# Two heads to a task: K tiles that hold half of each of two heads, and V in rows of 8 KB

## The chip, the cores and the metric

One core of a Trainium2 chip runs the whole program. The metric is the device time of one execution in microseconds; before the change three runs took 1159.95, 1160.93 and 1161.16 us, median 1160.93.

The five engines are TensorE (PE, with PEld for its weight loads), VectorE (DVE), ScalarE (ACT), GpSimd (POOL) and SyncE (SP). SP issues every DMA of this kernel, in one queue and in order; 16 DMA engines move the bytes.

## What is computed

A decode step of a transformer with two layers, each attention and an MLP, both layers with the same weights and the same K and V caches. There are 8 sequences (batches) with one new token each, width 512, 32 query heads in 8 groups on 8 K/V heads, 8192 cached positions, head size 128, all bf16.

```python
def _A_ref(x, k_cache, v_cache, wq, wo):          # k_cache, v_cache: (8, 8, 8192, 128)
    q = (x @ wq).reshape(B, Sq, Hq, Dh).transpose(0, 2, 1, 3)
    k = jnp.repeat(k_cache, 4, axis=1)
    v = jnp.repeat(v_cache, 4, axis=1)
    p = _softmax(jnp.einsum("bhqd,bhkd->bhqk", q, k) * (Dh ** -0.5), axis=-1)
    o = jnp.einsum("bhqk,bhkd->bhqd", p, v)
    return o.transpose(0, 2, 1, 3).reshape(B, Sq, Hq * Dh) @ wo
def _B_ref(x, w1, w2):
    return _silu(x @ w1) @ w2                     # 512 -> 1792 -> 512
for _layer in range(2):
    x = x + _A_ref(_layernorm(x), k_cache, v_cache, wq, wo)
    x = x + _B_ref(_layernorm(x), w1, w2)
```

K and V of one batch and head are 2 MB each. All K and V together are 268 MB, and layer 2 needs them again.

## The kernel before

**Tasks and positions.** A task is one layer, batch and K/V head: 2 x 8 x 8 = 128 tasks. A task has 8 *positions* (GPT); two positions make a *granule* (GPG), and a task has four granules, each 2048 cached keys. The program is one loop over positions p (L1010 of the listing), which emits for all engines what belongs to p.

**The arena.** K and V land in ARENA, 28 slots of 512 KB (4 KB in each of 128 partitions). A granule of K or of V takes one slot. Of each batch, K of heads 3 to 7 (20 granules) is *kept* in the arena from layer 0 until layer 1 has scored it, so it is read once; heads 0 to 2 are read in both layers. The kept K of heads 3 to 7 in layer 0 comes as one load of 2 MB with 16 KB rows. V of a granule is one load of 512 KB with 4 KB rows.

**Order of tasks** (`make_tasks`). For each batch b: layer 0 of heads 3 to 7 (here the *kept stretch*: wide K and V are loaded), then some five tasks of heads 0 to 2, of layer 0 of later batches and layer 1 of earlier ones (the *middle stretch*: K and V in 512 KB loads), then layer 1 of heads 3 to 7 (the *late stretch*: V alone is loaded, and kept K is given back). The chain from layer 0 to layer 1 of a batch (wo, residual, layer norm, w1, silu, w2, residual, layer norm, wq; some twenty stages, one or more in a position) runs within the middle stretch.

**Loads** (`plan_loads`). Every load has a position `need` at which it is used and one, `free`, at which its slot comes free. Loads are sorted by `need`; each gets the slot that comes free first and a position `after` from which it may be issued. SP issues in this order (`issue_until`), and waits where the slot is still in use; what stands behind it waits too. K is needed a position ahead of its granule, V LP = 14 positions behind it.

**One task.** K of a granule is transposed in place in 32 x 32 blocks by VectorE (L497). PE multiplies it with the queries (L563) into one of two PSUM banks SCp; a bank is 128 x 512, its 64 used rows are (column group, granule, head of the group). After the last granule: row maximum (L574), its spread over the 4 query heads (L576), an all-reduce over partitions on POOL (L579), the shift (L583, L586), exp on ACT into P (L590), sums (L597, POOL L599), four transposes on PE into TPp (L608), copy to PT (L612). Then P times V (L628), a granule each time two positions have passed, into one of two banks OTp. The four column groups of the result are joined: ACT writes the first part into `joint` (L643), VectorE adds three (L651), PE folds the rows (L665), VectorE scales (L675). P and `joint` are the same tile E.

The positions of these steps within a task are fixed: softmax_max at 0 (of the next task's positions), shift and exp at 2, sum at 4, turning P at 5, reciprocal at 7; own at 6, join at 7, fold and norm at 1, each LP + GPT positions behind the task.

Of the kernel before, what the change touches and what calls it, by code (L numbers as in the profile page):

```python
# [19 lines left out]
READ = (1, 1, 1, 4, 4, 4, 4, 4)  # L20
KEEP = 20
LT = 1
PRE = 10
LP = 14
EARLY = 4
DEAL_AT = 30
WO_FROM = 36
NTP = 2
NSCP = 2
NPT = 1  # L30
# [12 lines left out]
NAT = 2  # L43
CW = 32
# [108 lines left out]

def make_tasks(nb, nkv, keep_from):
# [10 lines left out]
    na = 0  # L165
    for b in range(nb):
        if b:
            tasks += kept[b]
        size = -(-(2 * first * (nb - 1)) // nb) if b in (0, nb - 1) else 2 * first * (nb - 1) // nb
        must = max(0, first * min(b + 1, nb - 1) - na)  # L170
        nd = size if b == nb - 1 else min(len(behind), first, size - must)
        tasks += behind[:nd]
        del behind[:nd]
        take = ahead[na:na + size - nd]
        na += len(take)
        tasks += take
        if b + 1 == nb:
            tasks += behind
        tasks += c[b]
        behind += d[b]  # L180
# [4 lines left out]
def plan_loads(tasks, kept, nslot, ngran):  # L185
# [3 lines left out]
    for i, (layer, b, g) in enumerate(tasks):  # L189
        for k in range(ngran):  # L190
# [8 lines left out]
            loads.append(Load("V", b, g, k, i0 + GPG - 1 + LP, i0 + GPG - 1 + LP))  # L199
    loads.sort(key=lambda d: (d.need, d.kind))  # L200
# [8 lines left out]
    for d in loads:  # L209
        w = ngran if d.kind == "K" and (d.g, d.k) in kept else 1  # L210
        if w > 1 and d.k:
            d.slot = whole[d.g] + d.k
            d.after = by
            assert d.after < d.need or d.need == -1 and d.after == -2, (d.kind, d.need, d.after)
            continue
# [5 lines left out]
        for m in range(w):  # L221
            free[d.slot + m] = d.free
        if w > 1:
            whole[d.g] = d.slot
# [19 lines left out]
def _build(ctx, nc, A_x, A_k_cache, A_v_cache, A_wq, A_wo, B_w1, B_w2, out):  # L244
# [43 lines left out]
    def half(slot, h):  # L288
# [8 lines left out]
    XT = [sb([128, KT, B], BF16, f"XT{n}") for n in range(3)]  # L297
# [5 lines left out]
    QT2 = [sb([128, HQ], BF16, "QT2") for _ in range(2)]  # L303
# [12 lines left out]
    hsT = sb([128, FT * B], BF16, "hsT")  # L316
    xnT = sb([128, KT, B], BF16, "xnT")
    s1 = sb([128, B], FP32, "s1")
    s1a = sb([128, B], FP32, "s1a")
    s2 = sb([128, 1], FP32, "s2")  # L320
    s2a = sb([128, 1], FP32, "s2a")
    top = sb([128, REP], FP32, "top")
    tops = sb([128, REP], FP32, "tops")
    ssm = [sb([128, REP], FP32, "ssm") for _ in range(NST)]
    ssa = [sb([128, REP], FP32, "ssa") for _ in range(NST)]
    widths = {"own_q": NQ, "hm": REP, "far": REP, "mine": REP, "own_x": XW, "real": 1, "rowmax": 1,
              "eps": 1, "shift": 1, "eh": FT, "vr": B, "yr": B, "tr": B}
    widths.update({f"rcp{n}": REP for n in range(NST)})
    widths.update({f"rs{n}": 1 for n in range(NST)})
    row = sb([128, sum(widths.values())], FP32, "row")  # L330
    tiny, at_col = {}, 0
    for name, w in widths.items():
        tiny[name] = row[:, at_col:at_col + w]
        at_col += w
    own_q, hm, far, mine, own_x, real, rowmax, eps, shift, vr, yr, tr = (
        tiny[n] for n in ("own_q", "hm", "far", "mine", "own_x", "real", "rowmax", "eps", "shift", "vr", "yr", "tr"))
    rcp = [tiny[f"rcp{n}"] for n in range(NST)]
    rs = [tiny[f"rs{n}"] for n in range(NST)]

# [58 lines left out]
    def issue(d):  # L398
        cache = A_k_cache if d.kind == "K" else A_v_cache
        if d.kind == "K":  # L400
            src = cache[d.b, d.g].rearrange("(p k c) d -> k p (c d)", k=NGRAN // d.wide, p=128)[d.k // d.wide]
        else:
            src = cache[d.b, d.g].rearrange("(k p c) d -> k p (c d)", k=NGRAN, p=128)[d.k]
# [7 lines left out]
    with nc.Block() as block:  # L411

        @block.sync
        def _(sync_eng):
# [13 lines left out]
                    hm[:, :], lanes.rearrange("p c (k r) -> p r c k", k=NGRAN), AX.XY, ALU.add),  # L428
                reads=["ident"], writes=["hm"],
            )  # L430
            op(
# [7 lines left out]
            for n in range(NSCP):  # L439
                op(dve, lambda n=n: dve.memset(SCp[n][:, :], 0.0), writes=[f"SC{n}"])  # L440
            op(dve, lambda: dve.tensor_reduce(real[:, :], hm[:, :], AX.X, ALU.add), reads=["hm"], writes=["real"])
# [3 lines left out]
            op(dve, lambda: dve.tensor_scalar(  # L445
                far[:, :], hm[:, :], real[:, 0:1], FAR, op0=ALU.subtract, op1=ALU.mult),
               reads=["hm", "real"], writes=["far"])
# [57 lines left out]

            span_of = {}
# [10 lines left out]
            def emit_queries(layer, b):  # L517
                if layer == 0:
                    q, rq = QT1[:, b * HQ:(b + 1) * HQ], f"QT1_{b}"
                else:  # L520
                    q, rq = QT2[b % 2][:, :], f"QT2_{b % 2}"
# [9 lines left out]
            def emit_q(ti):  # L531
                layer, b, g = tasks[ti]
                if ti == span_of[(layer, b)][0]:
                    emit_queries(layer, b)
                n = ti % NQB
                at = qset[(layer, b)] * NPART * HQ
                op(dve, lambda: dve.tensor_tensor(  # L537
                    QB[n][:, :, :].rearrange("p i (a r) -> p i a r", a=NQ),
                    QSp[:, at:at + NPART * HQ].rearrange("p (i h) -> p i h", h=HQ)[:, :, g * REP:(g + 1) * REP].unsqueeze(2)
                    .to_broadcast([128, NPART, NQ, REP]),  # L540
                    own_q[:, :].unsqueeze(1).unsqueeze(3).to_broadcast([128, NPART, NQ, REP]), ALU.mult),
                   reads=["QS", "own_q"], writes=[f"QB{n}"])

            def emit_s(i):
# [9 lines left out]
                bank, qn = ti % NSCP, ti % NQB  # L554
# [17 lines left out]
            def softmax_max(ti):  # L572
                bank = ti % NSCP
                op(dve, lambda: dve.tensor_reduce(rowmax[:, :], SCp[bank][:, :], AX.X, ALU.max),  # L574
                   reads=[f"SC{bank}"], writes=["rowmax"])
# [434 lines left out]
            for p in range(NG + LP + GPT + FOLD + 1):  # L1010
# [22 lines left out]
                if 0 <= ti < ntask and ph in soft:  # L1033
                    for f in soft[ph]:
                        f(ti)
# [62 lines left out]
```

## Time and profile before

| | |
|---|---|
| median of three runs | 1160.93 us |
| the profiled execution, its own time | 1159.96 us |
| its span, first to last instruction | 1157.8 us |
| what lies around the span | 2.2 us |
| busy: PE, PEld, DVE, ACT, POOL | 725.2, 346.7, 740.8, 336.6, 116.7 us |
| mean granted TensorE clock | 0.596 of full speed |
| HBM read | 465.05 MB, 402 GB/s over the span |
| transposes of K (L497) | 352, 1235 ns each |
| exp (L590) | 128, 1421 ns each (with the read of its sum) |
| row maximum (L574) | 128, 659 ns each |
| all-reduces on POOL (L579, L599) | 128 and 128, 371 and 436 ns each |

How to read it: busy time is the time in which an engine has an instruction at work, over the whole span; the page also gives it in 40 equal slices as digits, tenths of a slice. A group's line has the line of the code, engine, operation, what it writes and reads, the count, its busy time, the mean of one, and then the engine's idle time just ahead of it with what ended that idle time. A DMA group has KB of one load and the median time from issue to landing. In the list of waits stand the waiting engine and line, the releaser, the total, how often, and the longest.

### The profile page before, as it was taken

To read this page: it belongs to the slowest core of one execution; us is meant where nothing else is said; L and a number is where in the kernel's file an instruction comes from. 1 tells how busy PE (TensorE), PEld (TensorE's weight loads), DVE (VectorE), ACT (ScalarE), POOL (GpSimd) and SP (SyncE) were. 2 spreads that over 40 slices of the span, in tenths; PEclk is the share of its full clock that TensorE was granted. 3 is DMA by queue.
4 is the path that set the end of the run, shared out by engine and by line. 5 is a ranking of instruction groups with operands and counts; after the bars stand their busy time and mean duration, and the time that the engine had idled before them with its cause. 6 is when DMAs were issued, how large, how long until landed. Compare 5 with 4: busy or idle time off the path is not lost.

```text
span 1157.8 us, 26616 instructions
## 1 busy us (share of the span) xinstructions
PE 725.2 (63%) x10768; PEld 346.7 (30%) x10768; DVE 740.8 (64%) x1781; ACT 336.6 (29%) x764; POOL 116.7 (10%) x296
## 2 busy tenths in 40 slices
PE   1445677566765676567756676567665677567666
PEld 1212342123322342134322342134222332134224
DVE  3836764676557675677467765677477755677464
ACT  0352224223332233122422233222332233223332
POOL 0000011001110111001100011001100011001110
PEclk9855556555765566555755576555755565556665
DMA  9999999999999999999999999999999999999994
GB/s 372 403 400 415 408 408 414 417 411 404 407 419 415 402 407 417 419 401 409 408 416 411 409 401 416 417 407 403 406 419 410 409 401 419 414 408 403 409 408 184
DMA packets 112602, 466.80 MB, mean 403 GB/s; under 512 B 11984, under 2 KB 16096, under 8 KB 106720
## 3 DMA queue, kind: packets, MB, share of 16 engines
q1 hardware_dynamic: 112480, 465.11, 100.1%
q8 instruction: 85, 1.39, 0.5%
q14 instruction: 37, 0.30, 0.1%
HBM read 465.05 MB, written 0.01 MB: 402 GB/s over the span
## 4 chain that ended last, share of the span: by engine, by line
DMA 53%; DVE 15%; PE 13%; SPq 9%; issue 6%; ACT 3%; POOL 1%; DVEq 0%; ACTq 0%; POOLq 0%
DMA arena<-in_A_v_cache_dram 36%; DMA arena<-in_A_k_cache_dram 17%; SPq L379 9%; DVE arena L497 6%; DVE E L651 4%; PE OTp L628 4%; PE SCp L563 3%; DVE row L574 2%; PE TPp L608 2%; PE OTp L665 1%; PE MISC L762 1%; ACT E L590 1%; PE MISC L780 1%; ACT PT L612 1%; DVE top L576 1%
## 5 line engine op out<-in xcount | busy, mean ns | idle before, releaser
L497 DVE STREAM_TRANSPOSE arena<-arena 128x1024 int32<-128x1024 int32 x352 | 433.3, 1235 | 162.2 <-DMA arena<-in_A_k_cache_dram 161.9
L628 PE MATMUL OTp<-arena,PT 128*16 128x512 bf16 (+1 forms) x2064 | 278.5, 550 | 292.3 <-DMA arena<-in_A_v_cache_dram 271.3
L590 ACT ACTIVATE E<-SCp,row 128x512 bf16<-128x512 f32 x128 | 181.9, 1421 | 605.9 <-DVE row L586 587.2
L563 PE MATMUL SCp<-arena,QB 128*16 128x128 bf16 (+1 forms) x4352 | 251.1, 375 | 22.6 <-DVE arena L497 16.3
L651 DVE SCALAR_TENSOR_TENSOR E<-OTp,row,E 128x128 f32<-128x128 f32 x381 | 130.2, 342 | 113.6 <-ACT E L643 103.1
L628 PEld LDWEIGHTS OTp<-arena,PT 128*16 128x16 bf16 (+1 forms) x2064 | 51.2, 92 | 422.0 <-DMA arena<-in_A_v_cache_dram 382.6
L563 PEld LDWEIGHTS SCp<-arena,QB 128*16 128x16 bf16 x4352 | 100.8, 110 | 112.2 <-issue 59.2
L579 POOL PARTITION_ALL_REDUCE tops<-top x128 | 47.5, 371 | 587.7 <-DVE top L576 439.0
L608 PE MATMUL TPp<-ident,E 128*128 128x128 bf16 x512 | 72.7, 291 | 37.6 <-ACT E L590 36.2
L599 POOL PARTITION_ALL_REDUCE ssa<-ssm x128 | 55.8, 436 | 350.2 <-ACT ssm L597 350.2
L574 DVE TENSOR_REDUCE row<-SCp 128x1 f32<-128x512 f32 x128 | 84.4, 659 | 0.7 <-PE SCp L563 0.7
L612 ACT COPY PT<-TPp 128x256 bf16<-128x256 bf16 x128 | 47.7, 372 | 125.0 <-PE TPp L608 125.0
L665 PE MATMUL OTp<-row,E 128*128 128x4 f32 x254 | 68.9, 342 | 23.3 <-DVE E L651 23.2
L665 PEld LDWEIGHTS OTp<-row,E 128*128 128x128 f32 x254 | 57.8, 283 | 82.9 <-DVE E L651 47.3
L608 PEld LDWEIGHTS TPp<-ident,E 128*128 128x128 bf16 x512 | 41.1, 124 | 111.5 <-ACT E L590 89.5
L780 PE MATMUL MISC<-at,wo 128*128 128x32 bf16 x1024 | 37.4, 188 | 18.8 <-DVE row L583 14.7
L643 ACT ACTIVATE E<-OTp,row 128x128 f32<-128x128 f32 x127 | 47.2, 372 | 0.0
L762 PE MATMUL MISC<-xnT,wq 128*128 128x32 bf16 (+1 forms) x1152 | 35.8, 186 | 14.2 <-DVE xnT L749 13.9
L762 PEld LDWEIGHTS MISC<-xnT,wq 128*128 128x128 bf16 x1152 | 34.8, 105 | 20.8 <-issue 18.6
L780 PEld LDWEIGHTS MISC<-at,wo 128*128 128x128 bf16 x1024 | 32.9, 105 | 25.4 <-DVE at L675 22.3
L597 ACT ACTIVATE ssm<-row 128x4 f32<-128x4 f32 x128 | 37.9, 296 | 3.8
L537 DVE TENSOR_TENSOR QB<-QSp,row 128x64 bf16<-128x64 f32 x128 | 25.7, 201 | 17.6 <-PE QSp L524 17.5
(100 smaller groups left out, 319.3 us busy)
## 6 DMA issues: line engine op xcount, KB each, us to landing
arena<-in_A_v_cache_dram SPq DMA_DIRECT2D x512, 512.0 KB, 10.5
arena<-in_A_k_cache_dram SPq DMA_DIRECT2D x192, 512.0 KB, 8.3
arena<-in_A_k_cache_dram SPq DMA_DIRECT2D x40, 2048.0 KB, 22.5
wq<-in_A_wq_dram SPq DMA_DIRECT2D x1, 4096.0 KB, 16.3
wo<-in_A_wo_dram SPq DMA_DIRECT2D x1, 4096.0 KB, 36.9
w<-in_B_w_dram SPq DMA_DIRECT2D x2, 1792.0 KB, 25.0
E<-in_A_x_dram SPq DMA_DIRECT2D x1, 8.0 KB
out_dram<-E SPq DMA_DIRECT2D x1, 8.0 KB
```

What stands on the lines that cost most here:

```text
L379: eng.dma_start(out_ap, in_ap).then_inc(counter.sem, 16)
L497: op(dve, lambda: dve.transpose(words, words), reads=[r_half(slot, 0), r_half(slot, 1)], writes=[r_half(slot, 0), r_half(slot, 1)])
L563: lambda n=n, t=t: pe.matmul(SCp[bank][t * QUAD:t * QUAD + USED, lo * 128:(lo + len(slots)) * 128], QB[qn][:, n, :], keys(t, n), start=(n ...
L574: op(dve, lambda: dve.tensor_reduce(rowmax[:, :], SCp[bank][:, :], AX.X, ALU.max), reads=[f"SC{bank}"], writes=["rowmax"])
L590: op(act, lambda: act.activation(P[:, :].rearrange("p (x j k) -> p k x j", x=CPB, k=NGRAN), SCp[bank][:, :].rearrange("p (k x j) -> p k x ...
L608: lambda c=c: pe.transpose(tpv[:, c, :], P[:, c * 128:(c + 1) * 128], ident[:, :])
L612: op(act, lambda: act.copy(PT[pb][:, :, :, :, :].rearrange("p a t x r -> p x t a r"), tpv.rearrange("p x (t q) -> p x t q", q=QUAD)[:, :, ...
L628: lambda t=t, y=y: pe.matmul(OTp[ob][t * QUAD:t * QUAD + w * REP, 0:w * DH], PT[pb][:, k, t, y * w:(y + 1) * w].rearrange("p x r -> p (x r)"),
L651: op(dve, lambda x=x: dve.scalar_tensor_tensor(joint, OTp[ob][:, x * DH:(x + 1) * DH], own_x[:, x:x + 1], joint, op0=ALU.mult, op1=ALU.add ...
L665: lambda: pe.matmul(OTp[ob][:, 0:REP], joint, hm[:, :], start=True, stop=True)
L762: lambda o=o, k=k: pe.matmul(MISC[:, o * n:o * n + w], w_sb[:, k, o * 128:(o + 1) * 128], rhs_of(k).to_broadcast([128, w]) if n == 1 else ...
L780: lambda o=o, h=h: pe.matmul(MISC[:, o * w:(o + 1) * w], wo_sb[:, h, o * 128:(o + 1) * 128], rhs_of(h).to_broadcast([128, w]) if n == 1 el ...
```

## The change

Heads 0 and 1, 4 and 5, 6 and 7 become pairs (DUOS); heads 2 and 3 stay alone. A pair is two tasks in a row.

- **K of a pair.** A K tile no longer holds 128 rows of one head. Partitions 0 to 63 hold rows of the first head, 64 to 127 rows of the second; a partition's whole row is 128 keys (32 KB) and a tile takes every eighth part of it (4 KB), or for kept K half of it (16 KB). So a pair's eight tiles together hold both heads, and none can be finished before both tasks are scored. The number and size of the K loads stay.
- **V of a pair** is loaded two granules at once: 1 MB with 8 KB rows, into two slots next to each other. The second slot comes free two positions after the first.
- **Scores** of a pair lie in two banks, so there are three (NSCP), and one bank TPp is given up, of which both halves are now used. A kept head of a pair is scored by `score_both` in two groups of 16 matmuls with 256 columns, in place of one group of 16 with 512.
- **Softmax** is done once for a pair, in the first eight positions after its second task: two row maxima, one all-reduce over 8 columns in place of two over 4, two exps through the same P with a turn between them, two copies to PT (NPT = 2). The sum of a pair is formed on VectorE and no longer on ACT. A head alone waits the same eight positions more.
- **Lags.** V lags 22 positions (LP) in place of 14. The queries of the first late task are now due at position 4 of that task (LATE), not 3 before it.
- **Order.** `make_tasks` doesn't part a pair; the middle stretches have 5, 6, 5, 5, 5, 6, 4 and 6 tasks, before 6, 5, 5, 5, 5, 5, 5 and 6.
- **Room.** XT has one buffer in place of three, QT2 one in place of two; small tiles move into `row`, E and a free slot of the arena.

The diff, cut to its core:

```diff
+DUOS = (0, 4, 6)
-LP = 14
+LP = 22
-NTP = 2
-NSCP = 2
-NPT = 1
+NTP = 1
+NSCP = 3
+NPT = 2
+LATE = 4
...
+def lead_of(g):
+    return g - 1 if g - 1 in DUOS else g
+
+def members(g):
+    return 2 if lead_of(g) in DUOS else 1
...
-            loads.append(Load("V", b, g, k, i0 + GPG - 1 + LP, i0 + GPG - 1 + LP))
-    loads.sort(key=lambda d: (d.need, d.kind))
+            w = members(g)
+            if k % w == 0:
+                loads.append(Load("V", b, g, k, i0 + GPG - 1 + LP, i0 + GPG - 1 + LP, w))
+    loads.sort(key=lambda d: (d.need, d.kind == "K" and d.wide == 1))
...
         for m in range(w):
-            free[d.slot + m] = d.free
+            free[d.slot + m] = d.free + (GPG * m if d.kind == "V" else 0)
...
         if d.kind == "K":
-            src = cache[d.b, d.g].rearrange("(p k c) d -> k p (c d)", k=NGRAN // d.wide, p=128)[d.k // d.wide]
+            rows = cache[d.b, lead:lead + n].rearrange("g (p f) d -> (g p) (f d)", p=128 // n)
+            at = own if d.wide > 1 else d.k * n + own
+            src = rows[:, at * d.wide * SLOT:(at + 1) * d.wide * SLOT]
         else:
-            src = cache[d.b, d.g].rearrange("(k p c) d -> k p (c d)", k=NGRAN, p=128)[d.k]
+            src = cache[d.b, d.g].rearrange("(k p c) d -> k p (c d)", k=NGRAN // n, p=128)[d.k // n]
...
+            def score_both(ti, slots, qn):
+                own = tasks[ti][2] - lead_of(tasks[ti][2])
+                cols = NGRAN // 2 * 128
+                many = ARENA[:, slots[0] * SLOT:(slots[0] + NGRAN) * SLOT].rearrange(
+                    "p (k u t x h j e) -> p u t h e k x j", u=2, t=NQ, x=CPB, h=PAIRS, e=2, j=QUAD)
+                for u in range(2):
+                    bank = (ti - own + u) % NSCP
+                    mm_group([
+                        lambda n=n, t=t: pe.matmul(
+                            SCp[bank][t * QUAD:t * QUAD + USED, own * cols:(own + 1) * cols], QB[qn][:, n, :],
+                            many[:, u, t, n // 2, n % 2], start=(n == 0), stop=(n == NPART - 1))
+                        for n in range(NPART) for t in range(NQ)
+                    ], reads=[r_half(slot, h) for slot in slots for h in range(2)] + [f"QB{qn}"], writes=[f"SC{bank}"])
...
+                for n in range(many):
+                    bank = (ti + n) % NSCP
+                    op(dve, lambda: dve.tensor_reduce(rowmax[:, n:n + 1], SCp[bank][:, :], AX.X, ALU.max),
+                       reads=[f"SC{bank}"], writes=["rowmax"])
+                if many > 1:
+                    op(dve, lambda: dve.tensor_tensor(rowmax[:, 0:1], rowmax[:, 0:1], rowmax[:, 1:2], ALU.max),
+                       reads=["rowmax"], writes=["rowmax"])
...
-            soft = {0: [softmax_max], 2: [softmax_shift, softmax_exp], 4: [softmax_sum], 5: [emit_pt], 7: [softmax_rcp]}
...
+            def softmax(ti, ph):
+                many = members(tasks[ti][2])
+                if ph == 0:
+                    softmax_max(ti)
+                elif ph == 2:
+                    softmax_shift(ti)
+                    softmax_exp(ti, 0)
+                elif ph == 3 and many > 1:
+                    emit_turn(ti, 0)
+                    softmax_exp(ti, 1)
+                elif ph == 4:
+                    softmax_sum(ti)
+                elif ph == 5:
+                    emit_turn(ti, many - 1)
+                    emit_pt(ti)
+                elif ph == 7:
+                    softmax_rcp(ti)
...
-                ob, pb = ti % 2, ti % NPT
+                ob, own, many = ti % 2, g - lead_of(g), members(g)
+                pb, at = (ti - own + k % many) % NPT, own * NGRAN // many + k // many
...
-                        PT[pb][:, k, t, y * w:(y + 1) * w].rearrange("p x r -> p (x r)"),
+                        PT[pb][:, at, t, y * w:(y + 1) * w].rearrange("p x r -> p (x r)"),
...
-                ti, ph = p // GPT - 1, p % GPT
-                if 0 <= ti < ntask and ph in soft:
-                    for f in soft[ph]:
-                        f(ti)
+                ti = p // GPT - 2
+                if 0 <= ti < ntask and lead_of(tasks[ti][2]) == tasks[ti][2]:
+                    softmax(ti, p % GPT)
                 if chain:
-                    left = max(1, first1[chain_b[0]] - EARLY - p)
+                    left = max(1, due_of[first1[chain_b[0]]] + LQ - EARLY - p)
```

`emit_turn` makes the four PE transposes of P that `emit_pt` made before, into one half of TPp; `emit_pt` copies one half or both to PT.

## The prediction

> **What bounds the kernel now.** I read the profiled execution from the outside in: slices, DMA queues, stretches, then the waits. The first two views say that the DMA engines never rest.
>
> ```profile
> span 1157.8 us, 26616 instructions
> ...
> DMA  9999999999999999999999999999999999999994
> GB/s 372 403 400 415 408 408 414 417 411 404 407 419 415 402 407 417 419 401 409 408 416 411 409 401 416 417 407 403 406 419 410 409 401 419 414 408 403 409 408 184
> DMA packets 112602, 466.80 MB, mean 403 GB/s; under 512 B 11984, under 2 KB 16096, under 8 KB 106720
> ...
> q1 hardware_dynamic: 112480, 465.11, 100.1%
> ...
> arena<-in_A_v_cache_dram SPq DMA_DIRECT2D x512, 512.0 KB, 10.5
> arena<-in_A_k_cache_dram SPq DMA_DIRECT2D x192, 512.0 KB, 8.3
> arena<-in_A_k_cache_dram SPq DMA_DIRECT2D x40, 2048.0 KB, 22.5
> ```
>
> No slice but the last falls below 90%, and q1 alone fills the 16 engines. No compute engine does: PE is 63% and VectorE (DVE) 64% busy. The waits point the same way:
>
> ```profile
> PEld OTp L628 <- DMA arena<-in_A_v_cache_dram: 382.6, 291, 16.8
> ...
> DVE arena L497 <- DMA arena<-in_A_k_cache_dram: 161.9, 83, 7.3
> ```
>
> P·V waits for V and the transposes for K. So the time is the packet work of the DMA queue, plus a start, plus the 14 us between the last data packet (1143.9 us) and the end. The rate isn't flat, and that is where the row length shows (columns: stretch, busy times, PE clock, DMA share, GB/s):
>
> ```profile
> 9.40:19.40 10.00, 0.24 (x4) 0.18 (x4) 2.93 (x12) 0.00 (x0) 0.28 (x1) 1.00 1.00 418
> 54.00:64.00 10.00, 0.00 (x0) 0.00 (x0) 0.59 (x1) 9.14 (x3) 0.00 (x0) 0.50 1.10 348
> 110.00:180.00 70.00, 49.62 (x904) 27.44 (x900) 47.83 (x115) 19.11 (x50) 7.57 (x19) 0.52 1.03 408
> 191.00:241.00 50.00, 28.53 (x270) 10.27 (x258) 31.54 (x70) 14.10 (x30) 4.43 (x11) 0.57 1.02 417
> ```
>
> These are wq (8 KB rows), wo (1 KB rows), K and V in 4 KB rows, and wide K (16 KB rows) with V, half and half.
>
> **1. V in 8 KB rows.** Six of eight heads are in pairs: 6 x 8 x 2 = 96 tasks, 384 loads of 512 KB, which become 192 of 1 MB: 201 MB. Per engine 3072 packets of 4 KB become 1536 of 8 KB, so 1536 go. Price of one packet, with one engine at a sixteenth of the rate: 4 KB at 408 GB/s is 160.6 ns. wo: 1 KB at 348 is 47.1 ns, and four of these less 160.6, over three packets, are 9.2 ns. Kept stretch: 157.2 ns per 4 KB at 417 means 153.8 for the 16 KB half, and 6.8 ns over three quarters of a packet are 9.1. wq: 313.6 ns per 8 KB at 418, against 321.2, is 7.6. The packet records have medians of 160 ns (4 KB) and 309 ns (8 KB): 11. So 7.6 to 11 ns, 11.7 to 16.9 us. I take 9.5, between wo's and the records: **-14.6 us**.
>
> The Trainium skill, "DMA: Bandwidth & Descriptors", section "Why small descriptors are slow (HBM only)", gives a packet a fixed overhead of some 3 cycles beside one per 32 B: 262 cycles for two packets of 4 KB, 259 for one of 8 KB. By it the 201 MB would save 1.1% of their 493 us, an estimate of 5.6 us. The four rows above all say more, so the trace doesn't agree.
>
> **2. K in halves.** The 32 tasks of heads 0 and 1 still read 4 KB rows, the kept ones 16 KB rows; only the row pitch doubles. K (16 KB pitch) and V (contiguous) land 1.28 us apart alike at 110 to 180 us, so I charge 0; 1 ns on each of 1024 packets per engine would be 1 us, either way.
>
> **3. The arena behind a pair.** This is the new risk. Twenty of 28 slots hold kept K, eight circulate. Carrying out the planner of both versions: in the middle stretch (heads 0 to 2 of either layer) the loads issued but not yet needed are a constant 7 slots before; after, they alternate between 5 and 7, since a pair is given back only when its second half is used, two positions on. One round is a V pair A and K tiles k1, k2: 2.49 + 2 x 1.28 = 5.05 us of DMA. A lands at 0, k1 at 1.28; k1 is transposed (1.24, L497), scored (0.60, L563), then A's second half is used (0.60, L628): with 0.2 of semaphores A is free at 3.9. VectorE may be late: from landing to the next issue on its slot a K tile is held 2.45, 3.11, 2.45 and 3.95 us in turn (trace, 112 to 135 us; V 0.74). The tiles that gate a pair are the first and third of a task, so up to 0.65 more: 4.6. Six slots (7.5 us) were queued when A landed, 2.9 us of them remain. A new load needs 1.04 us to its first packet and 0.72 us from last packet to count (first load: issued 0.79, first packet 1.83, first engine 3.83), so 1.1 us of cover is left at worst, 1.7 at best: **0 us** in a steady round. SP's queue is in order, so the K loads behind a pair wait with it; that is in these numbers.
>
> **4. The chain of stages to layer 1** (wo, MLP, query; once in each of the eight middle stretches) puts PE behind: at 797 to 809 us K is held 5.06 and 3.86, V 1.5 to 2.8, some 1.5 to 2 us over steady. That was hidden by a queue deeper by one slot; now it exceeds the cover by 0 to 0.9. I take 0.5 each, **+4 us**; bounds 0 and 14 (1.75 each, the whole mean lag). It now has 18 positions where it had 19 (due 4 after the first late task, start 8 later), once only 10.
>
> **5. Softmax in pairs.** Two exponentials share one P buffer: PE's first turn waits for exp 0, exp 1 on ScalarE (ACT) for that turn; the next K score and P·V queue behind it on PE, and SP waits for those. In the middle stretch two positions take 2.57 us against 1.43 + 0.27 + 0.6 (L590, L608), so nothing stalls. In the late stretch (layer 1, heads 3 to 7) compute sets its own pace, 5.7 us a task:
>
> ```profile
> 824.83 1.12 DVE L651 SCALAR_TENSOR_TENSOR E<-OTp,row,E 128x128 f32<-128x128 f32 x3 [2.85 <-ACT E L643]
> 825.87 0.17 DVE L619 RECIPROCAL row<-ssa 128x4 f32<-128x4 f32 x1
> 825.96 0.66 DVE L574 TENSOR_REDUCE row<-SCp 128x1 f32<-128x512 f32 x1
> 826.65 0.22 DVE L576 SCALAR_TENSOR_TENSOR top<-row 128x4 f32<-128x4 f32 x1
> ...
> 830.57 1.13 DVE L651 SCALAR_TENSOR_TENSOR E<-OTp,row,E 128x128 f32<-128x128 f32 x3 [2.71 <-ACT E L643]
> ```
>
> From join to join 5.74 us. For a pair, by the same rows: join to exp 0 2.65 (two reductions), exp 1.5, turn 0.65, score and P·V 2.5 over exp 1, turn 0.65, PT copies, own and join 2.25; then fold, two P·V and score 3.7, own and join 1.5: 15.4, 7.7 a task. It costs **0** because each such task frees 8 slots (4 V, 4 kept K), 10 us of DMA work. If these stretches freed only V, 2.7 us x 32 paired tasks would be 86 us.
>
> **6. The rest.** POOL's 256 all-reduces become 160 and SP's V issues 320; the masks, the moved constants and the three-to-one XT run beside transfers: 0. The tail of V alone is 22 positions instead of 14, behind a slower late stretch: 0 to 3 us if compute is last there, I take **+1**.
>
> Sum: 1159.96 (span 1157.8 and 2.2 around it) - 14.6 + 4 + 1 = 1150.4. The median of the runs is 1.0 above the profiled one: **1151**; its own range 1146 to 1156.
>
> **Rivals.** (a) Nothing given back and the packet records right: 1160.9 - 16.9 = 1144. For it: the cover in part 3. Against: 4 KB stretches already dip to 380 GB/s in chains. 0.20. (b) Starved behind pairs: the second reduction (0.66) comes before the transposes, and a held k1 keeps two slots. It decides once K is held over some 4.2 us on the mean, since 1.28 + 4.2 + 0.6 leaves 1.4 us queued where 1.76 are needed; at 4.3 us 0.4 us fall idle in each of some 80 rounds, 32 us: 1161 - 14.6 + 5 + 32 = 1183, and on the way there anything over 1163. For it: 3.95 occurs steadily already, 5.06 in chains. Against: those aren't the gating tiles. 0.18. (c) The chains cost their upper 14: 1160.9 - 14.6 + 14 + 1 = 1161, no change. 0.07. (d) The gain isn't there: rows beyond some length run alike, wq was fast because nothing else ran, and the 417 comes from longer DMAs; then 1161 + 5 = 1166. Against: wo and the packet records. 0.07. The same skill page, section "Specifications", speaks for it: line rate from 512 B on. By that rule no row here would change; the trace disagrees at wo's 1 KB, 348 against 408.
>
> **How the numbers follow.** The forecast has 0.48, so faster is 0.48 + 0.20 = 0.68; same (within 0.2%, 2.3 us, which a measurement of this kernel can't tell apart) 0.07; slower 0.18 + 0.07 = 0.25. The range runs from 1142, below (a) by the K pitch's 1 us and a little, to 1168, past (c) and (d) and into the light end of (b); outside lie most of (b) and a few hundredths below, under 0.2.
>
> **What would show it.** Packets fall by some 27,600; V issues show 192 of 1024 KB and 128 of 512. In the kept stretches GB/s rises from 417 to about 422, in stretches of V alone from 408 to about 420. Wrong in part 3: slices of the middle stretches below 400 GB/s with a DMA share under 1. Wrong in part 5: falling GB/s in the kept stretch after a late one, when the freed slots are used up. Wrong in part 1: 408 where V goes in 8 KB rows.

## The result and the profile after

The changed kernel takes 1204.24 us (median of four runs, 1202.35 to 1207.96) against 1161.05 in the same session: a ratio of 1.0378, interval 1.0365 to 1.0391. It is 43 us slower, where 10 us less had been forecast. The profiled execution is the one of 1202.35 us. Its page, the lines that answer to those of before:

```profile
span 1200.5 us, 27836 instructions
...
DMA  9999999999999999999999999999999989999994
GB/s 375 401 410 389 388 381 424 419 376 387 373 423 407 373 367 423 422 375 385 410 422 386 358 360 429 416 393 398 375 426 410 369 325 427 417 387 381 385 414 170
DMA packets 84956, 466.87 MB, mean 389 GB/s; under 512 B 8912, under 2 KB 13024, under 8 KB 54496
...
q1 hardware_dynamic: 84832, 465.10, 97.1%
...
arena<-in_A_v_cache_dram SPq DMA_DIRECT2D x192, 1024.0 KB, 9.0
...
arena<-in_A_v_cache_dram SPq DMA_DIRECT2D x128, 512.0 KB, 8.6
```

The bytes are the same and 27,646 packets are gone, so V does go in 8 KB rows. But q1 no longer fills the engines: 97.1% of the span, which is 43 us longer. The digits of the DMA row hardly show it, the GB/s row does: slices of 423 to 429 beside slices of 325 to 375. The stretches tell them apart (columns as before: stretch, busy times of PE, PEld, DVE, ACT and POOL, PE clock, DMA share, GB/s):

```profile
180.00:240.00 60.00, 32.38 (x436) 15.87 (x436) 39.38 (x82) 14.65 (x29) 3.15 (x8) 0.61 1.01 422
240.00:280.00 40.00, 21.62 (x404) 11.67 (x400) 25.39 (x50) 8.77 (x20) 2.35 (x6) 0.54 0.99 371
300.00:320.00 20.00, 12.59 (x218) 6.68 (x214) 7.97 (x27) 4.93 (x11) 1.11 (x3) 0.79 0.88 343
...
960.00:990.00 30.00, 18.11 (x434) 12.30 (x434) 12.45 (x44) 8.76 (x27) 3.17 (x8) 0.73 0.85 325
```

A kept stretch runs at 422 GB/s, as forecast. A middle stretch (240 to 280) runs at 371 with a share of 0.99, the start of a late stretch (300 to 320) at 343 with 0.88, and the one behind the middle stretch of four tasks (960 to 990) at 325 with 0.85. In an undisturbed stretch the share reads 1.01 to 1.03, as it did before the change in the same stretch:

```profile
240.00:280.00 40.00, 24.56 (x417) 12.81 (x418) 30.32 (x63) 10.44 (x26) 4.01 (x10) 0.54 1.03 408
```

That it is 0.99 at 371 GB/s means that packets take longer here (8 KB packets 357 ns on the mean, against 313 in 180 to 240 us), so it can't be read as work done.

To say where time went I added up the packets. Each counts with what it takes in an undisturbed stretch (by the rates there and the records of both traces: 46.9 ns for 1 KB, 160.6 for 4 KB, 311.7 for 8 KB, 614 for 16 KB, other sizes in between; the few that load instructions count too), a sixteenth of it since 16 engines share them. So counted, the packets of 110 to 180 us before the change fill 69.9 of 70 us, and those of 315 to 360 us after it 45.1 of 45. What a stretch is longer than its packets is lost. "Late starts" are eight windows from 12 us ahead of the end of a chain of stages to 13 us behind it; "ahead of them" is the 33 us before each; "other" is what remains up to the last load; "end" what follows that. The kernels e1 to e12 are those of the next section.

| kernel | span | packets | start | late starts | ahead of them | other | end |
|---|---|---|---|---|---|---|---|
| before | 1157.8 | 1136.0 | 2.9 | 2.4 | 1.1 | 1.7 | 13.9 |
| after | 1200.5 | 1121.6 | 3.0 | 25.0 | 20.7 | 14.1 | 16.4 |
| e1 | 1179.0 | 1136.2 | 3.5 | 16.6 | 1.2 | 4.9 | 16.9 |
| e2 | 1182.3 | 1121.6 | 3.6 | 22.1 | 8.2 | 10.7 | 16.3 |
| e3 | 1186.4 | 1121.5 | 3.6 | 18.5 | 16.1 | 12.2 | 14.7 |
| e7 | 1164.5 | 1121.6 | 3.4 | 21.8 | 1.1 | 1.0 | 15.7 |
| e8 | 1142.1 | 1109.6 | 3.6 | 5.0 | 0.3 | 4.2 | 19.7 |
| e9 | 1178.0 | 1121.6 | 3.6 | 19.3 | 7.1 | 10.2 | 16.3 |
| e10 | 1178.0 | 1126.5 | 3.3 | 2.2 | 10.2 | 17.6 | 18.4 |
| e11 | 1155.9 | 1126.5 | 3.5 | 4.9 | 2.9 | 4.1 | 14.1 |
| e12 | 1174.3 | 1121.6 | 3.6 | 27.9 | 0.4 | 6.2 | 14.8 |

(Rows add up to within 0.3; with slightly other edges of the windows a column moves by up to 0.8.) The change did save 14.4 us of packets. It lost 54.6 more in the middle of the run (59.8 in three columns against 5.2), and 2.5 at the end.

What a steady middle stretch looks like inside is in two views. First DMA in 40 slices of 0.55 us, 240 to 262 us:

```profile
DMA  9696999989999879998999997799989999769998
GB/s 425 246 343 246 462 380 417 417 365 387 395 425 410 298 253 402 447 432 320 417 387 380 387 320 223 290 417 417 372 343 372 447 380 484 313 283 387 439 320 335
```

Then the loads that SP issued then (start, duration, engine, line; an issue that waits for its slot isn't counted as busy, so what shows is when it got through):

```profile
240.31 0.33 SPq L394 DMA_DIRECT2D arena<-in_A_v_cache_dram  x1
240.69 3.32 SPq L394 DMA_DIRECT2D arena<-in_A_k_cache_dram  x2
246.10 0.33 SPq L394 DMA_DIRECT2D arena<-in_A_v_cache_dram  x1
246.48 2.52 SPq L394 DMA_DIRECT2D arena<-in_A_k_cache_dram  x2
250.23 0.33 SPq L394 DMA_DIRECT2D arena<-in_A_v_cache_dram  x1
...
256.17 0.33 SPq L394 DMA_DIRECT2D arena<-in_A_v_cache_dram  x1
```

A pair of V goes out every 4 to 6 us and 1 to 4 us behind each, at 247 to 248, 253 and 259 us, the engines dip to 220 to 315 GB/s. By the landing records the pair issued at 246.10 went out just when the pair before it had landed (246.04). Two K tiles hadn't landed yet, but of their packets only 1.3 us were *still to begin* (packets of the loads issued by then whose records start later, each with its time from above). The pair landed 5.18 us after its issue: these 1.3, its 2.49 of transfer, and 1.4 more. The first packets of the pair issued at 250.23 began at 252.8; of the first eight, five took 0.9 to 1.5 us, where the median of 8 KB packets in a kept stretch is 0.31. Pairs were held 3.7 to 5.0 us, K tiles up to 5.4.

The second place is the late start (start, duration, engine, line, what; in brackets the idle time just before and what ended it):

```profile
302.66 10.48 SPq L394 DMA_DIRECT2D arena<-in_A_v_cache_dram  x5
...
304.34 0.39 PE L709 MATMUL OTp<-arena,PT 128*16 128x512 bf16 x4
...
306.85 1.39 ACT L642 ACTIVATE E<-SCp,row 128x512 bf16<-128x512 f32 x1 [4.11 <-DVE row L638]
...
308.30 0.61 PE L667 MATMUL TPp<-ident,E 128*128 128x128 bf16 x4 [3.57 <-ACT E L642]
...
309.50 1.89 PE L606 MATMUL SCp<-arena,QB 128*16 128x512 bf16 x16 [0.35 <-DVE QB L563]
...
311.17 0.61 PE L709 MATMUL OTp<-arena,PT 128*16 128x512 bf16 x4
```

PE's first turn of the pair stands 3.57 us for exp 0; behind it on PE come the queries, the wide score (1.89 us) and only then P·V. From 304.34 to 311.17 no V is used, so none of its slots comes back. The list of waits says how much of that there is (waiting engine and line, releaser, total, times, longest):

```profile
PEld TPp L667 <- ACT E L642: 195.5, 107, 4.3
...
PE TPp L667 <- ACT E L642: 136.5, 93, 3.8
DVE arena L516 <- DMA arena<-in_A_k_cache_dram: 133.5, 78, 16.2
...
DVE row L655 <- ACT E L642: 118.2, 46, 3.9
...
PEld OTp L709 <- DMA arena<-in_A_v_cache_dram: 49.6, 35, 9.8
```

P·V's wait for V has gone from 382.6 to 49.6 us: V no longer comes last. PE's wait for the exponentials has grown from 36.2 (its old line L608) to 136.5, and VectorE stands 118 us at the sum of pairs (L655). In 240 to 264 us the compute engines wait for the DMA too, so this list alone doesn't say which wait starves which.

### The profile page after: what moved, and what is told of

Same layout as the page of the kernel before. It is cut to its first block, busy times and chain, and to the rows that moved or that the text cites. A ratio compares the mean times of both kernels' runs of the same rounds, so it can differ in the third digit from the quotient of the medians.

```text
span 1200.5 us, 27836 instructions
## 1 busy us (share of the span) xinstructions
PE 687.4 (57%) x11792; PEld 375.4 (31%) x11792; DVE 739.1 (62%) x1687; ACT 308.7 (26%) x668; POOL 77.7 (6%) x200
## 3 DMA queue, kind: packets, MB, share of 16 engines
q1 hardware_dynamic: 84832, 465.10, 97.1%
## 4 chain that ended last, share of the span: by engine, by line
DMA 37%; DVE 24%; PE 17%; issue 10%; ACT 9%; POOL 1%; SPq 1%; DVEq 0%; ACTq 0%; POOLq 0%
DMA arena<-in_A_k_cache_dram 36%; DVE arena L516 9%; ACT E L642 6%; DVE E L732 6%; DVE row L620 4%; PE OTp L709 4%; PE SCp L578 4%; PE TPp L667 3%; PE SCp L606 3%; PE MISC L851 2%; DMA arena<-in_A_v_cache_dram 1%; PE OTp L746 1%; ACT PT L674 1%; ACT E L724 1%; DVE row L626 1%
## 5 line engine op out<-in xcount | busy, mean ns | idle before, releaser
L709 PE MATMUL OTp<-arena,PT 128*16 128x512 bf16 (+1 forms) x2064 | 268.4, 551 | 49.5 <-DMA arena<-in_A_v_cache_dram 35.8
L606 PE MATMUL SCp<-arena,QB 128*16 128x128 bf16 (+1 forms) x3328 | 137.3, 310 | 115.8 <-DVE arena L516 95.5
L667 PE MATMUL TPp<-ident,E 128*128 128x128 bf16 x512 | 74.4, 296 | 137.7 <-ACT E L642 136.5
L578 PE MATMUL SCp<-arena,QB 128*16 128x256 bf16 x2048 | 108.9, 377 | 39.4 <-DVE arena L516 31.1
L606 PEld LDWEIGHTS SCp<-arena,QB 128*16 128x16 bf16 x3328 | 68.0, 108 | 176.5 <-DVE arena L516 136.5
L667 PEld LDWEIGHTS TPp<-ident,E 128*128 128x128 bf16 x512 | 42.1, 126 | 207.7 <-ACT E L642 195.5
L746 PE MATMUL OTp<-row,E 128*128 128x4 f32 x254 | 64.6, 325 | 59.5 <-DVE E L732 58.6
L709 PEld LDWEIGHTS OTp<-arena,PT 128*16 128x16 bf16 (+1 forms) x2064 | 58.4, 107 | 89.3 <-DMA arena<-in_A_v_cache_dram 49.6
L578 PEld LDWEIGHTS SCp<-arena,QB 128*16 128x16 bf16 x2048 | 59.5, 112 | 83.0 <-DVE arena L516 46.9
L655 DVE SCALAR_TENSOR_TENSOR row<-row 128x8 f32<-128x8 f32 x48 | 10.9, 228 | 118.2 <-ACT E L642 118.2
L629 POOL PARTITION_ALL_REDUCE row<-row x80 | 30.1, 376 | 693.9 <-DVE row L626 558.7
L674 ACT COPY PT<-TPp 128x256 bf16<-128x256 bf16 x128 | 43.0, 375 | 68.2 <-PE TPp L667 68.1
L658 POOL PARTITION_ALL_REDUCE row<-row x80 | 33.9, 424 | 298.5 <-DVE row L655 139.5
L563 DVE TENSOR_TENSOR QB<-QSp,row 128x32 bf16<-128x32 f32 (+1 forms) x128 | 23.7, 188 | 18.5 <-PE QSp L547 16.9
## 6 DMA issues: line engine op xcount, KB each, us to landing
arena<-in_A_k_cache_dram SPq DMA_DIRECT2D x40, 2048.0 KB, 16.1
```

The source lines that it names most:

```text
L578: lambda n=n, t=t: pe.matmul(SCp[bank][t * QUAD:t * QUAD + USED, own * cols:(own + 1) * cols], QB[qn][:, n, :], many[:, u, t, n // 2, n % ...
L606: lambda n=n, t=t: pe.matmul(SCp[bank][t * QUAD:t * QUAD + USED, lo * 128:(lo + len(slots)) * 128], QB[qn][:, n, :], keys(t, n), start=(n ...
L667: lambda c=c: pe.transpose(tpv[:, c, :], P[:, c * 128:(c + 1) * 128], ident[:, :])
L674: op(act, lambda: act.copy(PT[pb][:, :, :, :, :].rearrange("p a t x r -> p x t a r"), tpv.rearrange("p x (t q) -> p x t q", q=QUAD)[:, :, ...
L709: lambda t=t, y=y: pe.matmul(OTp[ob][t * QUAD:t * QUAD + w * REP, 0:w * DH], PT[pb][:, at, t, y * w:(y + 1) * w].rearrange("p x r -> p (x ...
L746: lambda: pe.matmul(OTp[ob][:, 0:REP], joint, hm[:, :], start=True, stop=True)
```

## The experiments

Four theories. **A**: the arena is too shallow behind a pair: with eight circulating slots, two given back at once and late, the queue runs dry in every round. **B**: PE stands at a pair's turns (L667), what is queued behind them comes late, and with it the slots. **C**: K rows at a pitch of 32 KB read worse. **D**: VectorE stands at the pair's sum (L655) ahead of the transposes of K. In the diffs "-" is the changed kernel.

**e1, V of a pair as two loads of 512 KB**, each into its own slot, rows of 4 KB as before; tasks, lags and softmax stay.

```diff
...
             src = cache[d.b, d.g].rearrange("(k p c) d -> k p (c d)", k=NGRAN // n, p=128)[d.k // n]
+            src = src[:, d.k % n * SLOT:(d.k % n + 1) * SLOT]
```

> V of a pair is loaded as two loads of 512 KB with 4 KB rows (8 KB apart), each slot given back on its own; K in halves, softmax in pairs and the lag of 22 stay. Theory A (the arena is too shallow behind a pair: a pair of slots is held 3.7 to 5 us and the queue behind it runs dry in every round of the middle stretches, some 4 us a batch, 32 us): these 32 us go, the row gain of some 15 us goes too, and the dips at the start of the late stretches stay: 1175 to 1190. Theory B (PE stands at the first turn of a pair's P, at the start of the late stretches above all, and with it every slot's release): nothing but the row gain changes, 1205 to 1220. Theory C (K rows 32 KB apart are slow to read): the same, 1205 to 1220.

**e2, both halves of a V pair used together**, at the first one's position, and given back together.

```diff
-            free[d.slot + m] = d.free + (GPG * m if d.kind == "V" else 0)
+            free[d.slot + m] = d.free
...
-                    emit_pv(p - LP)
+                    i = p - LP
+                    many = members(tasks[i // GPT][2])
+                    if i % GPT // GPG % many == 0:
+                        for m in range(many):
+                            emit_pv(i + GPG * m)
```

> Both halves of a V pair are used at the position of the first, so that both slots come free together, two positions earlier; 8 KB rows and all else stay. A: a pair is held about 1.4 us in place of 4.3, the middle stretches lose little, 1168 to 1180, and their slices rise above 400 GB/s. B: 1195 to 1204. C: 1200 to 1204.

**e3, one exponential and one turn of each pair left out**: both heads then take P and the sum of one bank.

```diff
...
-                    softmax_exp(ti, 0)
-                elif ph == 3 and many > 1:
-                    emit_turn(ti, 0)
-                    softmax_exp(ti, 1)
+                    softmax_exp(ti, many - 1)
```

> Leaves out the first exp of each pair and its turn, so that P is written once for a pair and PE waits for one exp only (both copies to PT take the same half). A: the middle stretches stay as they are, the dips at the late stretches shrink by the 2.1 us of one exp and turn: 1185 to 1198. B: most of the 59 us over 1145 go: 1150 to 1175. C: 1196 to 1204.

**e4, the old pitch of K**: the load takes the source of the kernel before, 16 KB from row to row, so a tile has other keys in it.

```diff
-            src = rows[:, at * d.wide * SLOT:(at + 1) * d.wide * SLOT]
+            src = cache[d.b, d.g].rearrange("(p k c) d -> k p (c d)", k=NGRAN // d.wide, p=128)[d.k // d.wide]
```

> K tiles hold 128 rows of one head again, 16 KB apart, as before the change, so that the scores are of other keys; sizes, order and everything else stay. A and B: no change, 1200 to 1207. C: 1150 to 1180.

| | median us | ratio to before, interval |
|---|---|---|
| e1 | 1183.32 | 1.0186, 1.0171 to 1.0201 |
| e2 | 1184.35 | 1.0203, 1.0163 to 1.0243 |
| e3 | 1190.36 | 1.0255, 1.0238 to 1.0273 |
| e4 | 1208.53 | 1.0402, 1.0378 to 1.0426 |

e4 gains nothing, so C falls. e1 lands where A had it. It pays the whole row gain back (1136.2 us of packets) and is still 21 us faster than the changed kernel: single slots take the loss ahead of the late starts from 20.7 to 1.2, and "other" from 14.1 to 4.9. That is A's share. e2 keeps the rows and takes the loss ahead of the late starts to 8.2: it matters that a pair comes back at once, though the time is 4 us above what A had set for e2. But in both the late starts still lose 16.6 and 22.1, so A isn't all. e3 shortens PE's and ACT's work at the pair's softmax and gains 14 us, in all three columns: B has a part too, but leaving work out says little about where it lies.

**e5, e6: the sum of a pair at position 6 and not 4**, behind the last turn; e5 in the changed kernel, e6 in e2.

```diff
-                elif ph == 4:
-                    softmax_sum(ti)
                 elif ph == 5:
                     emit_turn(ti, many - 1)
                     emit_pt(ti)
+                elif ph == 6:
+                    softmax_sum(ti)
```

> The sum of a softmax is formed at position 6 in place of 4, behind the second turn, so that VectorE no longer waits for the second exp of a pair with transposes queued behind it (118 us of idle time ahead of that instruction in the changed kernel). Theory D (this wait delays K's transposes and scores, and with them the slots): 1188 to 1196. Theory A alone (only the pair's slots held for two positions count): 1202 to 1206.

> Both halves of a V pair at one position, and the sum at position 6. A and D add up: 1166 to 1174. A alone: 1180 to 1186, as with both halves alone.

**e7, e2 with the exponentials and turns two positions later** (exp 0 at 4, turn 0 and exp 1 at 5, turn 1 at 7, sum at 8, reciprocal at 9), V lagging 24 positions.

```diff
-LP = 22
+LP = 24
...
-                    softmax_exp(ti, 0)
-                elif ph == 3 and many > 1:
+                elif ph == 4:
+                    softmax_exp(ti, 0)
+                elif ph == 5 and many > 1:
                     emit_turn(ti, 0)
                     softmax_exp(ti, 1)
-                elif ph == 4:
-                    softmax_sum(ti)
-                elif ph == 5:
+                elif ph == 7:
                     emit_turn(ti, many - 1)
                     emit_pt(ti)
...
```

> Both halves at one position; exp, turns and copies come two positions later (exp 0 at 4, first turn and exp 1 at 5, second turn at 7, sum and reciprocal in the next two), V lags 24. PE and VectorE then wait less for exp. Theory B' (PE's waits for the two exps delay P times V and so the slots): 1155 to 1168. A alone: 1180 to 1186. D without B': as the kernel with the sum at 6, 1166 to 1174.

**e8, 36 slots**: the changed kernel with eight slots more, which have room because wo isn't loaded; its projections read wq's tile. Packets of 12 us are saved with it.

```diff
-NSLOT = 28
+NSLOT = 36
...
```

> The changed kernel with 36 slots in place of 28; the room comes from leaving wo out (wq's memory is read in its place, its 4 MB aren't loaded, 12 us of the queue). Lack of depth, whatever holds the slots: the 58 us that the queue loses in the middle shrink to under 12, 1204 - 12 - 46 and more, 1130 to 1146. If the engines are too slow for the stream (pace, not depth): 1160 to 1192.

| | median us | ratio to before, interval |
|---|---|---|
| e5 | 1204.28 | 1.0372, 1.0354 to 1.0389 |
| e6 | 1182.89 | 1.0194, 1.0179 to 1.0209 |
| e7 | 1166.10 | 1.0051, 1.0036 to 1.0066 |
| e8 | 1143.03 | 0.9847, 0.9832 to 0.9862 |

e5 is the changed kernel to 0.04 us, e6 is e2 to 1.5: the 118 us that VectorE stands at L655 cost nothing that can be seen, and D falls. A long row in the list of waits was not a cause.

e8 is 61 us faster than the changed kernel, 49 of it beyond wo's packets, with the same softmax and no less waiting at the turns (154.7 us in all, one wait of 17.7 among them, against 136.5). Its GB/s row, in 40 slices of the span:

```profile
GB/s 362 422 418 416 412 419 423 416 415 411 421 421 415 414 416 423 418 413 411 415 420 415 414 392 423 417 412 415 419 421 416 414 374 424 416 414 413 414 415 73
```

With a deeper arena no slice of the middle but two falls below 411. So PE's stand and the pairs' late return are not a limit of pace; they cost time because eight slots can't bridge them. The Trainium skill, "Perfetto Trace Analysis", section "Optimization Strategy", reads a gap that repeats over a stretch on the engine that should be full as a possible want of room for the next tile; the dips every 4 to 6 us and e8 agree.

e7 is 18 us faster than e2. The dips of 240 to 262 us are gone but for one slice of 343 (the same view as above, now of e7):

```profile
DMA  9999999899998999999999999999999999999999
GB/s 439 410 425 402 410 387 410 343 417 372 454 439 365 417 439 380 372 410 425 425 365 432 410 402 395 425 425 425 425 439 425 417 425 372 425 410 432 432 425 425
```

What e7 still loses is the late starts, 21.8 of the 23.9 us between start and end, and 7.3 of it in one, behind the stretch of four tasks. Since e7 changes the lag and the turns' place together, two more kernels part them.

**e9, e2 with the turns one position later** (exp 0 at 3, turn 0 and exp 1 at 4, turn 1 at 6, sum at 7, reciprocal at 8), lag 22. Within a position the softmax's steps now also come ahead of own, join and fold, where they stood behind them.

```diff
-                    softmax_exp(ti, 0)
-                elif ph == 3 and many > 1:
+                elif ph == 3:
+                    softmax_exp(ti, 0)
+                elif ph == 4 and many > 1:
                     emit_turn(ti, 0)
                     softmax_exp(ti, 1)
-                elif ph == 5:
+                elif ph == 6:
                     emit_turn(ti, many - 1)
                     emit_pt(ti)
...
```

> Both halves of a V pair used together, and the exps and turns only one position later (exp 0 at 3, exp 1 at 4, the last turn at 6), so that V keeps its lag of 22. If PE's stand at a pair's turns is what loses time (1184 without any shift, 1166 with two positions), one position gives about half of it: 1172 to 1177. If half of that gain were due to the longer lag of V, and not to the wait, it stays at 1180 to 1184. If one position is enough to cover the wait, the chain has its two positions back and it comes out at 1160 to 1166.

**e12, e7 with the turns one position earlier**, where e9 has them, but with the lag of 24.

```diff
...
-                elif ph == 4:
+                elif ph == 3:
                     softmax_exp(ti, 0)
-                elif ph == 5 and many > 1:
+                elif ph == 4 and many > 1:
                     emit_turn(ti, 0)
                     softmax_exp(ti, 1)
-                elif ph == 7:
+                elif ph == 6:
                     emit_turn(ti, many - 1)
```

(Here "-" is e7; sum and reciprocal stay at 8 and 9.)

> The kernel that lost least with three pairs (1166: both halves together, V lag 24, exps and turns two positions later), with the exps and turns one position earlier again. The lag of 24 and with it the place of join and fold (after the row maximum on VectorE, not before it) stay; what goes is the granule of scores and P x V that PE had ahead of each turn. If the turns' place on PE is what counts, it returns to 1180 to 1184, as the kernel with the same order of turns and a lag of 22 (1180). If the join's place or the lag itself is what counts, it stays at 1164 to 1170.

| | median us | ratio to before, interval | PE's wait at the turns |
|---|---|---|---|
| e2 | 1184.35 | 1.0203, 1.0163 to 1.0243 | 141.3 |
| e9 | 1180.14 | 1.0153, 1.0133 to 1.0173 | 143.7 |
| e12 | 1178.43 | 1.0152, 1.0135 to 1.0169 | 89.9 |
| e7 | 1166.10 | 1.0051, 1.0036 to 1.0066 | 39.8 |

I had expected 1172 to 1177 from e9, half of e7's gain, and got 4 us over e2, which the intervals of the two don't tell apart. The reason is visible in its timeline: a position is a place in each engine's order, not a time. PE has scores and P·V at odd positions only, so a turn moved from 3 to 4 and one from 5 to 6 stand behind the same instructions as before, and the wait is the same. In e7 a turn at 5 or 7 has one more score (and at 5 P·V) ahead of it, and exp 0 runs meanwhile. e12 parts the two edits. With the lag of 24, at which the join of the task before comes behind the row maxima on VectorE and no longer ahead of them, it takes as long as e9, near the 1180 to 1184 set for the turns' place: the loss ahead of the late starts is gone (0.4 after 7.1), but the late starts lose 27.9 after 19.3. PE's wait at the turns falls from 143.7 to 89.9 without a gain in time, so that wait can't be read as time lost either. From e12 to e7, the turns alone, is 12.3 us by the medians and 9.8 by the profiled executions, of which 6.1 lie in the late starts and 5.2 in "other". The wait for the exponentials falls with it:

```profile
PEld TPp L667 <- ACT E L642: 137.3, 108, 1.8
```

```profile
PEld TPp L667 <- ACT E L642: 68.9, 59, 1.5
```

(e12 above, e7 below, in the list of waits; the changed kernel had 195.5, 107, 4.3.) So of B the turns' place is shown.

**e10, the changed kernel with heads 0 and 1 alone; e11, e7 with heads 0 and 1 alone.** Pairs 4+5 and 6+7 remain; no stretch has four tasks.

```diff
-DUOS = (0, 4, 6)
+DUOS = (4, 6)
```

> The changed kernel with heads 0 and 1 alone again (pairs 4+5 and 6+7 stay), so that no pair is among the tasks that read K and V into the eight circulating slots, but for the V of heads 6 and 7 at the start of each middle stretch. 64 pairs of V rows fewer: 128 loads of 1 MB in place of 192, so the row gain is 9.6 in place of 14.4. If the shallow arena behind the pairs of the middle stretches is where the time goes (some 40 of the 58 us lost in the middle), it falls to about 1204 + 5 - 35 = 1174. If the late starts and the pairs of kept heads lose most of it, it stays over 1195.

> The same two pairs, with both halves used together and the exps and turns two positions later (V lags 24). Row gain 9.6. The late starts lost some 13 us in the kernel with three pairs and these two edits, 7 of it at the middle stretch of four tasks, which this order doesn't have: 1161 - 9.6 + 6 = 1157 if that holds, 1166 or more if the losses at the late starts have to do with the longer lag alone.

e10 takes 1179.02 (1.0150, 1.0131 to 1.0168), e11 1158.78 (0.9984, 0.9974 to 0.9994; 12 runs, 1156.74 to 1163.59, against 17 of before, 1160.37 to 1162.25). In e10 the late starts lose 2.2 us, as before the change, though their tasks are pairs: what starved them came with the pairs 0+1 ahead of them (in the late start shown above, 302 to 313 us, the exps and turns are those of the pair that ends the middle stretch). What of such a pair does it is not shown: its V in single loads (e1) still leaves 16.6 us, and the order without pairs 0+1 has other middle stretches too, though in the changed kernel the one of four tasks has only 6.3 of the 25.0. What e10 still loses (10.2 and 17.6) is not at the late starts but ahead of them, and e11, with both edits of e7, takes these to 2.9 and 4.1. Its page has the same digits as before the change, at fewer packets:

```profile
DMA packets 94174, 466.89 MB, mean 404 GB/s; under 512 B 9936, under 2 KB 14048, under 8 KB 71904
...
q1 hardware_dynamic: 94048, 465.10, 99.3%
```

Two thirds of the row gain are 9.5 us of packets (1136.0 - 1126.5), and 7.5 of them are lost again (29.5 in its row against 22.0). e11 beats both kernels, the old one by 0.16%: the interval excludes 1, but it is less than the 0.2% named ahead as what can be told.

## Why the prediction was wrong, step by step

**Part 1, the rows: right.** Forecast 14.6, measured 14.4 from the packets, with 8 KB packets at 311.7 ns against twice 160.6: 9.5 ns a packet, the value taken; the 0.2 us between the two are instructions, of which a little more is loaded. The kept stretch went to 422, as said. The estimate of 5.6 us by the Trainium skill ("DMA: Bandwidth & Descriptors", "Why small descriptors are slow (HBM only)") is refuted here by that measurement, and with it rival (d).

**Part 2, the pitch: right.** e4 brings nothing.

**Part 3, the arena behind a pair: this step failed.** "0 us in a steady round" became 32.0 of the 54.6 us: 34.8 lost outside the late starts, against 2.8 before. The sign named for it is there, 371 GB/s at a share of 0.99. The held time was sized about right (a median of 3.7 us, forecast 3.9 to 4.6). Both other terms of the cover were wrong.

The larger one is the queue: "Six slots (7.5 us) were queued when A landed, 2.9 us of them remain." For the 62 pairs between 100 and 1060 us whose K neighbours, four loads to either side, are all of 512 KB, I added up the packets still to begin. At a pair's landing these are 4.6 us on the median, not 7.5, nor the 6.8 that remain of 7.5 without the 0.72 set apart for landing: only 13 of the 62 have six slots on the way, and part of such slots has been moved already. When a pair's V goes out, 2.2 us are left, 0.65 at the least, where before the change V loads between such neighbours went out with 5.05, 3.37 at the least. In the other kernels it is 3.2 and 0.7 (e2), 3.8 and 1.9 (e7), 9.4 and 5.8 (e8), and what they lose outside the late starts is least where the queue never ran low: 34.8 in the changed kernel, then 18.9, 2.1 and 4.5. Why the queue is so shallow is argued and not shown: in SP's order a late pair holds up the K loads behind it, whose slots are then late as well, so one round's delay is the next round's.

The smaller one is "a new load needs 1.04 us to its first packet and 0.72 us from last packet to count". It took the first of the 16 engines to count its part as landed (3.83 us). The last one of that load counted at 4.74, 2.7 us beyond the 1.28 of its transfer. Two pairs went out with 0.02 us still to begin, at 311.87 and 969.42; they landed 4.88 and 4.81 us later, 2.4 and 2.3 beyond their transfer. That alone would have left some 0.5 us of the 1.1 of cover. The Trainium skill, "DMA: Bandwidth & Descriptors", section "Anatomy of one DMA — SWDGE (gpsimd) path", gives a load some 2.0 us of fixed cost, most of it completion. It is for another issuing path, but nearer to these 2.3 to 2.4 than the 1.76 I had. That most of it is completion this trace doesn't show: the pair at 311.87 waited 0.96 us for its first packet and counted 0.31 us behind the end of its last.

**Part 4, the chain: right in its place, wrong in its cause and size.** Losses do gather at the end of the chains, 25.0 us in the late starts against 2.4, more than the 14 that bounded it. But the chain alone was not the cause: e10 has the same chains and loses 2.2.

**Part 5, softmax in pairs: failed at "nothing stalls".** I set the two exps and the turn against the length of two positions, as if exp 0 started with its position. It starts when row maxima, all-reduce and shift are through, and PE's turn, next in order, waits: 136.5 us in all and up to 3.8 each. Moving the turns, from e12 to e7, is worth 12.3 us. The rest of that part held: a pair in a late stretch takes 13.9 us (7.0 a task; 7.7 was worked out), and there the freed slots do cover it, since from 315 to 360 us the packets, summed by 5 us, lose nothing. What was overlooked is the first late task, where slots from kept K have not come back yet.

**Part 6**: the end took 2.5 us more, forecast 1, bounds 0 to 3.

**The rivals.** (b) named the direction and the place, starved behind pairs. Its condition wasn't met: it set in once K is held over 4.2 us on the mean, and K of heads 0 to 2 was held 3.8 (3.4 before). The engines starved at such holds because the queue was shallower than the forecast and the rival had it. Its 32 us are the 32.0 lost outside the late starts, but by another sum (0.4 us in each of 80 rounds at a hold of 4.3): that is luck. The 20 us beyond its 1183 are the late starts, 22.6 more than before where it had 4, and 1.5 at the end.

**What stays open**: why e3, with less work at the softmax, gains only 4.6 us ahead of the late starts, where e7's order, over e2, takes nearly all that is left there (8.2 to 1.1). And e7 against e2 has the place of the join in it, which was tried only together with the lag. What of a pair 0+1 starves the late starts is open too: five of the eight middle stretches end with head 2 and not with a pair, and their late starts lose 1.8 to 6.3 us, those behind a pair 2.5 to 3.6.

## What to carry to other kernels

Larger rows buy their packets' overhead (9.5 ns each here) at any depth, but a larger load that comes back later takes queue depth, and the depth that counts is the packets still to begin when the slot is given back, read from the trace and not from the plan's slots, less the load's own time from issue until its last engine has counted. When a DMA-bound kernel gains packets and loses time, add up the packets at their undisturbed durations and place the rest by stretch: it separates the gain from the stalls, which no share of busy time did here. And a wait is moved by giving the waiting engine other work ahead of it, not by a later number in a schedule: e9 moved little but the numbers, e7 moved the work.

## What the hardware showed that I had not expected

A 1 MB load that went out with 0.02 us of packets still to begin needed 2.3 to 2.4 us beyond its transfer (311.87 and 969.42 us; the first load of the run before the change, 512 KB, needed 2.7). Some 0.95 us pass to its first packet, and its first 16 packets take 0.3 to 1.2 us each where 0.31 is usual. The busy share of the DMA engines hides this: 0.99 in a stretch that runs at 371 GB/s where 408 went before with smaller packets.
